# Eighty-row loads, batch 2 with paired local loads and padded keys, and a new order, in a sparse attention and ELU expert kernel

## The chip, the cores and the metric

The kernel runs on one core of a Trainium2 chip. The core has five engines with a queue each: TensorE (PE) multiplies matrices, VectorE (DVE) and ScalarE (ACT) work element by element, GpSimd (POOL) here mostly issues the loads, and SyncE (SP) issues the transposing copies and the stores. The metric is the time of the whole kernel on the device in microseconds (us), the median over its runs; lower is better.

## The reference

Attention over 8 batches, 8 heads, 576 positions of 64 numbers, in float32. The first four heads see the last 32 positions, the other four every position of the same residue modulo 32. The result goes through two layers with an ELU between them.

```python
scores = (q @ k.T) / sqrt(64)
local   = (rel >= 0) & (rel < 32)                        # heads 0 to 3
strided = (rel >= 0) & (pos_k % 32 == pos_q % 32)        # heads 4 to 7
x = softmax(where(mask, scores, -1e9)) @ v               # 4608 tokens x 512
h = x @ w_in                                             # 512 x 2048
g = where(h > 0, h, exp(min(h, 0)) - 1)
out = g @ w_out                                          # 2048 x 512
```

## The kernel before

**Attention.** A position is split into a residue of 8 (NS) and one of 72 rows (RS). A unit of attention is a pair of heads: `0s1` is batch 0, strided, pair 1; `2l0` is batch 2, local, pair 0. Each pair goes through two halves (u = 0, 1), and each step of it is a token of the text ORDER:
- `l.` load of q, k or v by POOL, cast to bf16 (`qs`, `ks`, `vs` strided, `ql`, `kl`, `vl` local, then the batch, and a or b for half the heads); `wi`, `wo` are quarters of the two weights
- `T` transposes on PE (line 370), `c` and `C` the copies of their result out of PSUM by DVE or ACT (line 386); `D` and `K`, instead of these, the transposing copy on SP (line 557) and the copy into padded keys (line 568)
- `S` scores (line 399), `e` the exponential on ACT, `m` the mask on DVE, `O` the product with v (line 494), `n` the logarithm of the sums, `r` its negative exponential (both ACT), `x` the scaled result into xT (line 524, DVE)
- `A`, `F`, `z` set-up; `V`, `W` copies of v; `w` idle matmuls on zeros that fill PE.

A token's last number names PSUM banks: there are eight in all, and a token that writes a bank waits for the last reader of what lay there before.

**Three kinds of batch.** Batches 0, 1 and 2 (PE_T) have their transposes on PE; there the scores of the two pair members use half of the array's rows each (`Pair.rows`). For their local heads, one transpose of half width is made for each head and each of the 8 residues: 16 a token. Batches 3 to 7 use D and K: q lies in qTs, qTl, shared by all batches; k in kTs, kTl and from there in kps, kpl, in which the other head's rows are zero, so that the scores use all rows. A batch's D.qs thus waits for the last scores of the batch before. D.qs needs 80 rows (RP) for 72; the set-up A.r (line 320) fills the 8 spare rows once. Batches 0 and 1 add the sums by products with ones (`pv_old`); batches 2 to 7 take them along with v (V_ONES).

**The two layers.** Tokens go in 9 chunks of 512. For each of 16 slices m: `a` and `b` (or `L`) are the four matmuls of layer 1 (line 574), `h` the exponential on ACT, `i` (DVE) or `j` (ACT) the clamp, `g` the ELU's join on DVE. Layer 2 is `Z`, four matmuls a token (line 609); `o` (ACT) or `q` (DVE) copies the result, `t` stores it. Layer 1 of chunk 0 starts with the strided half of x (`a`) and adds the local half (`b`).

**What sets the order.** ORDER is written out in full by a planner and executed token by token; each engine gets its instructions in that order and waits only for the data it needs. SP's queue holds D, K and t, POOL's all loads.

Of the kernel before, what the change touches and what calls it, by code (L numbers as in the profile page):

```python
# [9 lines left out]
BF16 = mybir.dt.bfloat16  # L10
# [6 lines left out]
D = 64  # L17
# [14 lines left out]


# [7 lines left out]
A.i w.7.34 l.ks0b z.1 l.qs0b F.0 A.p F.2 l.qs0a z.0 l.ks0a z.2 l.kl0 F.1 T.0s1.k.0 w.7.5 A.m  # L41
l.ql0 C.0s1.k T.0s1.q.1 l.vs0 w.7.5 z.3 C.0s1.q l.vl0 T.0s0.q.0 w.7.1 C.0s0.q S.0s1.0.23
S.0s1.1.45 l.wi0 e.0s1.0 T.0s0.k.0 w.7.15 e.0s1.1 m.0s1.0 l.wo1 C.0s0.k m.0s1.1 l.wi1 T.0l1.k.1
l.wi2 S.0s0.1.67 c.0l1.k T.0l0.k.0 l.vs1 e.0s0.1 S.0s0.0.23 C.0l0.k m.0s0.1 l.wi3 T.0l1.q.1
e.0s0.0 A.l T.0l0.q.7 C.0l1.q m.0s0.0 w.6.3 O.0s1.0.2345 C.0l0.q O.0s1.1.2345 S.0l0.0.01 n.0s1
S.0l1.0.67 r.0s1 l.wo0 e.0l1.0 x.0s1 e.0l0.0 l.ks1 S.0l0.1.67 m.0l1.0 S.0l1.1.23 m.0l0.0 l.qs1
e.0l0.1 O.0s0.0.0145 V.0 e.0l1.1 O.0s0.1.0145 l.ql1 m.0l0.1 m.0l1.1 O.0l1.0.2367 n.0s0 l.qs2
r.0s0 O.0l1.1.2367 l.kl1 x.0s0 n.0l1 l.vl1 r.0l1 O.0l0.0.0145 O.0l0.1.0145 l.wo2 x.0l1 n.0l0
l.wo3 a.0.0.2 r.0l0 a.0.1.3 l.ks2 a.0.2.6 x.0l0 a.0.3.7 l.ql2 l.vs2 b.0.0 b.0.1 l.kl2 h.0.0
a.0.4.0 h.0.1 b.0.2 i.0.0 l.vl2 g.0.0 b.0.3 h.0.2 b.0.4 j.0.2 a.0.5.2 a.0.6.1 j.0.1 g.0.2 b.0.5  # L50
h.0.4 g.0.1 b.0.6 h.0.5 a.0.7.6 i.0.4 b.0.7 h.0.6 i.0.5 a.0.8.3 g.0.4 h.0.7 b.0.8 g.0.5 h.0.3
a.0.9.0 i.0.7 b.0.9 h.0.8 g.0.7 a.0.10.2 h.0.9 b.0.10 i.0.3 j.0.8 g.0.3 a.0.11.6 a.0.12.4 h.0.10
g.0.8 b.0.11 j.0.10 i.0.6 b.0.12 i.0.9 h.0.11 a.0.13.3 g.0.9 a.0.14.7 h.0.12 g.0.10 b.0.13
j.0.12 b.0.14 g.0.6 j.0.11 a.0.15.2 g.0.12 b.0.15 h.0.14 T.1s0.k.5 g.0.11 j.0.14 T.1s0.q.4
c.1s0.k T.1s1.k.1 h.0.15 g.0.14 T.1s1.q.6 C.1s0.q Z.0.0.0.5 c.1s1.q h.0.13 i.0.15 c.1s1.k
S.1s0.0.67 g.0.15 S.1s0.1.01 e.1s0.0 i.0.13 T.1l1.q.4 e.1s0.1 g.0.13 S.1s1.1.67 c.1l1.q
T.2s1.q.0 m.1s0.1 e.1s1.1 S.1s1.0.12 m.1s0.0 T.2s0.q.4 c.2s1.q e.1s1.0 O.1s0.1.67 l.qs3 m.1s1.1
C.2s0.q m.1s1.0 O.1s0.0.01 A.r n.1s0.1 T.1l1.k.2 r.1s0.1 O.1s1.1.34 n.1s0.0 x.1s0.1 Z.0.0.1.5
r.1s0.0 C.1l1.k x.1s0.0 T.1l0.k.6 n.1s1.1 V.1 S.1l1.1.01 r.1s1.1 c.1l0.k T.1l0.q.2 e.1l1.1
x.1s1.1 O.1s1.0.67 c.1l0.q S.1l1.0.01 m.1l1.1 n.1s1.0 S.1l0.0.34 r.1s1.0 Z.0.0.2.5 e.1l1.0  # L60
x.1s1.0 e.1l0.0 m.1l1.0 S.1l0.1.67 O.1l1.1.01 m.1l0.0 e.1l0.1 O.1l1.0.23 n.1l1.1 m.1l0.1
O.1l0.0.67 n.1l1.0 Z.0.0.3.5 r.1l1.0 r.1l1.1 x.1l1.0 Z.0.1.0.4 n.1l0.0 x.1l1.1 o.0.0 T.2s1.k.0
r.1l0.0 Z.0.1.1.4 t.0.0 C.2s1.k x.1l0.0 Z.0.1.2.4 Z.0.1.3.4 O.1l0.1.23 q.0.1 Z.0.2.0.0 l.vl3
n.1l0.1 t.0.1 r.1l0.1 T.2s0.k.1 W.2 Z.0.2.1.0 l.ks3 C.2s0.k x.1l0.1 Z.0.2.2.0 l.vs3 Z.0.2.3.0
Z.0.3.0.1 q.0.2 Z.0.3.1.1 t.0.2 Z.0.3.2.1 Z.0.3.3.1 V.2 L.1.0.0 q.0.3 L.1.1.2 t.0.3 h.1.0
S.2s1.1.56 i.1.0 h.1.1 g.1.0 S.2s0.0.34 e.2s1.1 L.1.2.1 i.1.1 e.2s0.0 m.2s1.1 L.1.3.0 g.1.1
h.1.2 m.2s0.0 O.2s1.1.56 h.1.3 S.2s0.1.34 i.1.2 g.1.2 L.1.4.2 n.2s1.1 i.1.3 r.2s1.1 L.1.5.1
g.1.3 h.1.4 x.2s1.1 T.2l0.q.7 h.1.5 i.1.4 O.2s0.0.56 e.2s0.1 c.2l0.q T.2l0.k.0 g.1.4 n.2s0.0
S.2s1.0.34 m.2s0.1 r.2s0.0 L.1.6.2 D.qs c.2l0.k e.2s1.0 x.2s0.0 L.1.7.7 h.1.6 m.2s1.0 D.ks
O.2s0.1.34 i.1.5 h.1.7 S.2l0.0.56 g.1.5 L.1.8.0 n.2s0.1 i.1.7 r.2s0.1 g.1.7 T.2l1.q.1 e.2l0.0  # L70
x.2s0.1 T.2l1.k.7 l.ql3 h.1.8 m.2l0.0 O.2s1.0.56 c.2l1.q L.1.9.3 n.2s1.0 c.2l1.k K.s L.1.10.1
r.2s1.0 i.1.8 g.1.8 h.1.9 L.1.11.7 x.2s1.0 h.1.10 l.kl3 L.1.12.0 i.1.9 h.1.11 g.1.9 O.2l0.0.45
i.1.10 L.1.13.6 n.2l0.0 g.1.10 L.1.14.3 r.2l0.0 i.1.6 g.1.6 l.ks4 h.1.13 L.1.15.1 x.2l0.0 j.1.13
l.qs4 i.1.11 S.2l1.1.45 h.1.15 g.1.11 Z.1.0.0.2 e.2l1.1 i.1.15 g.1.13 h.1.14 S.2l1.0.45 m.2l1.1
h.1.12 S.2l0.1.67 i.1.14 Z.1.0.1.2 e.2l1.0 D.kl i.1.12 g.1.14 e.2l0.1 O.2l1.1.45 g.1.12
Z.1.0.2.2 n.2l1.1 D.ks m.2l0.1 S.3s0.1.67 r.2l1.1 g.1.15 e.3s0.1 x.2l1.1 O.2l0.1.01 D.ql n.2l0.1
S.3s0.0.67 m.3s0.1 S.3s1.0.34 m.2l1.0 Z.1.0.3.2 e.3s0.0 W.3 e.3s1.0 m.3s0.0 Z.1.1.0.7 l.kl4 K.l
q.1.0 r.2l0.1 O.3s0.1.56 m.3s1.0 O.3s0.0.34 t.1.0 x.2l0.1 n.3s0.1 Z.1.1.1.7 n.3s0.0 V.3
O.2l1.0.01 Z.1.1.2.7 r.3s0.0 r.3s0.1 l.vl4 x.3s0.0 Z.1.1.3.7 n.2l1.0 x.3s0.1 Z.1.2.0.2 l.vs4
r.2l1.0 q.1.1 O.3s1.0.34 l.ks5 x.2l1.0 S.3s1.1.56 t.1.1 n.3s1.0 Z.1.2.1.2 l.ql4 r.3s1.0 D.qs  # L80
S.3l0.0.01 L.2.0.7 e.3l0.0 x.3s1.0 e.3s1.1 m.3l0.0 L.2.1.0 K.s h.2.0 m.3s1.1 L.2.2.1 h.2.1 i.2.0
g.2.0 j.2.1 O.3s1.1.34 S.3l1.1.56 h.2.2 L.2.3.7 g.2.1 e.3l1.1 L.2.4.0 j.2.2 m.3l1.1 D.kl n.3s1.1
L.2.5.5 g.2.2 r.3s1.1 L.2.6.6 h.2.4 x.3s1.1 l.qs5 L.2.7.1 h.2.6 i.2.4 g.2.4 h.2.3 L.2.8.3 h.2.7
i.2.3 L.2.9.0 g.2.3 h.2.8 i.2.7 h.2.5 L.2.10.4 i.2.6 h.2.9 g.2.6 Z.1.2.2.2 j.2.9 i.2.5 g.2.7
h.2.10 S.3l1.0.67 Z.1.2.3.2 g.2.9 e.3l1.0 g.2.5 j.2.10 O.3l1.1.01 S.3l0.1.67 V.4 n.3l1.1
Z.1.3.0.5 K.l g.2.10 e.3l0.1 Z.1.3.1.5 m.3l1.0 r.3l1.1 m.3l0.1 O.3l0.0.67 o.1.2 x.3l1.1
Z.1.3.2.5 n.3l0.0 t.1.2 W.4 O.3l0.1.01 r.3l0.0 Z.1.3.3.5 i.2.8 l.vs5 n.3l0.1 x.3l0.0 L.2.11.2
r.3l0.1 q.1.3 O.3l1.0.67 D.ks x.3l0.1 h.2.11 L.2.12.4 l.vl5 n.3l1.0 i.2.11 L.2.13.5 g.2.11
# [24 lines left out]
x.5l0.1 L.4.9.3 h.4.8 i.4.7 t.3.3 L.4.10.0 g.4.7 j.4.8 K.s h.4.9 g.4.8 L.4.11.1 h.4.10 i.4.9
L.4.12.2 i.4.10 h.4.11 g.4.10 j.4.11 O.5s1.1.56 g.4.9 L.4.13.4 n.5s1.1 W.6 L.4.14.3 r.5s1.1
# [47 lines left out]
def kernel(  # L162
# [71 lines left out]
    def rawof(nm, b):  # L234
        return (raw1 if b == 1 else raw)[nm]
# [444 lines left out]
```

## Time and profile before

| | |
|---|---|
| median of 13 runs | 327.97 us (326.53 to 332.23) |
| the profiled execution | 326.53 us, its span 324.8 us |
| DVE, ACT busy | 228.9, 239.5 us |
| loads (q0) | 18.48 MB |
| transposes, K and stores (q1) | 18.95 MB |
| mean granted TensorE clock | 0.972 |
| end of the last matmul | 320.72 us |

A row of the timeline names start and length in us, engine, line, and how many instructions it merges; what stands in brackets is idle time before it and what ended it. A matmul's own duration (380 ns for 512 columns) is longer than the time from its start to the next one's start (216 ns), as they are pipelined; only the second can be added up. The landing of the loads is issue to last byte, so it holds the wait in the queue.

### The profile page before, as it was taken

What the parts mean: (1) busy time and instruction counts of PE and PEld (TensorE: products, weight loads), DVE (VectorE), ACT (ScalarE), POOL (GpSimd) and SP (SyncE); (2) the same over time, 40 slices, a digit from 0 to 9 for tenths busy, and PEclk for the clock granted to TensorE, in tenths of its full rate; (3) what the DMA queues carried; (4) which work ended last, traced back from release to release, by engine and by line L of the source; (5) the groups of instructions that cost most, each with busy time, mean ns of one, the idle gap of its engine ahead of it and who ended that gap; (6) DMA issues with size and microseconds to landing.
All of it is one profiled execution on the core that took longest, in us unless ns stands there. A gap on an engine that the chain in (4) does not pass through costs nothing.

```text
span 324.8 us, 6336 instructions
## 1 busy us (share of the span) xinstructions
PE 305.2 (94%) x2392; PEld 161.1 (50%) x2431; DVE 228.9 (70%) x423; ACT 239.5 (74%) x413; POOL 75.8 (23%) x105
## 2 busy tenths in 40 slices
PE   7869989989799999999999999998999999999994
PEld 6754554444355455554555444554544544444442
DVE  6655994399997999659686998854489569495010
ACT  3695986199798999789799988954898878592101
POOL 8753341305455041050513360000000000000000
PEclk9558999999999999999999999999999999999999
DMA  6999999937999999979999998129200210200332
GB/s 82 170 206 205 187 200 194 143 85 139 129 173 179 149 146 158 174 155 131 145 139 148 185 143 77 59 79 185 66 2 1 67 32 0 67 0 0 93 104 66
DMA packets 95663, 37.84 MB, mean 116 GB/s; under 512 B 76912, under 2 KB 89744, under 8 KB 95632
## 3 DMA queue, kind: packets, MB, share of 16 engines
q0 software_dynamic: 62576, 18.48, 55.2%
q1 hardware_dynamic: 33056, 18.95, 28.1%
q8 instruction: 19, 0.31, 0.4%
q14 instruction: 12, 0.10, 0.1%
HBM read 36.90 MB, written 9.44 MB: 143 GB/s over the span
## 4 chain that ended last, share of the span: by engine, by line
PE 61%; DVE 20%; ACT 9%; issue 4%; DMA 3%; POOL 1%; SPq 1%; ACTq 0%; POOLq 0%; DVEq 0%
PE ps L613 29%; PE ps L579 24%; DVE g L607 6%; DVE he L596 4%; ACT ln L516 3%; DVE g L605 3%; PE ps L418 3%; DVE xT L547 3%; ACT rc L522 2%; DMA kl<-in_k_dram 2%; PE ps L481 1%; ACT e L425 1%; DMA qTs<-qs 1%; PE ps L488 1%; DVE pm L438 1%
## 5 line engine op out<-in xcount | busy, mean ns | idle before, releaser
L579 PE MATMUL ps<-xT,w_in_sb 128*128 128x512 bf16 x560 | 130.5, 382 | 2.7 <-DVE g L607 0.7
L613 PE MATMUL ps<-w_out_sb,g 128*128 128x512 bf16 x553 | 131.2, 379 | 1.4 <-issue 0.3
L587 ACT ACTIVATE he<-ps 128x512 f32<-128x512 f32 x144 | 81.4, 591 | 23.2 <-PE ps L579 21.7
L579 PEld LDWEIGHTS <-w_in_sb 128*128 128x128 bf16 x576 | 55.5, 98 | 67.8 <-issue 6.0
L613 PEld LDWEIGHTS <-g 128*128 128x128 bf16 x576 | 53.1, 98 | 56.0
L607 DVE TENSOR_TENSOR g<-he,ps 128x512 bf16<-128x512 bf16 x89 | 60.5, 686 | 2.3
L547 DVE TENSOR_TENSOR xT<-ps,rc 64x576 bf16<-64x576 f32 (+2 forms) x60 | 42.7, 714 | 27.0 <-ACT rc L522 26.3
L425 ACT ACTIVATE e<-ps 72x576 bf16<-72x576 f32 (+1 forms) x64 | 39.9, 645 | 11.3 <-PE ps L418 10.6
L516 ACT ACTIVATE ln<-ps 64x576 f32<-64x576 f32 (+2 forms) x60 | 36.6, 613 | 13.4 <-PE ps L488 5.7
L596 DVE TENSOR_SCALAR he<-he 128x512 bf16<-128x512 f32 x89 | 37.9, 435 | 9.3 <-ACT he L587 8.9
L605 DVE SCALAR_TENSOR_TENSOR g<-he,ps 128x512 bf16<-128x512 bf16 x55 | 36.9, 683 | 7.6 <-ACT he L594 7.3
L522 ACT ACTIVATE rc<-ln 64x576 f32<-64x576 f32 (+2 forms) x60 | 38.8, 649 | 1.7
L594 ACT ACTIVATE he<-he 128x512 bf16<-128x512 f32 x55 | 34.1, 628 | 1.2
L619 DVE COPY osb<-ps 128x512 f32<-128x512 f32 x19 | 13.1, 688 | 27.9 <-PE ps L613 25.6
L619 ACT COPY osb<-ps 128x512 f32<-128x512 f32 x17 | 10.0, 586 | 24.7 <-PE ps L613 24.4
L248 POOL DMA_DIRECT2D ql<-in_q_dram x20 | 16.2, 816 | 26.6 <-PE ps L382 16.9
L255 POOL DMA_DIRECT2D kl<-in_k_dram x20 | 15.2, 776 | 17.9 <-DMA kTl<-kl 17.9
L432 DVE TENSOR_TENSOR pm<-e,mask_s 72x576 bf16<-72x576 bf16 x32 | 14.1, 449 | 4.2 <-ACT e L425 4.1
L438 DVE TENSOR_TENSOR pm<-e,mask_l 128x576 bf16<-128x576 bf16 x32 | 14.3, 454 | 3.4 <-ACT e L425 2.9
L263 POOL DMA_DIRECT2D vl<-in_v_dram x8 | 9.8, 1228 | 14.8 <-PE ps L466 6.5
L481 PEld LDWEIGHTS <-vsp 72*128 72x128 bf16 x192 | 9.1, 98 | 5.0 <-issue 0.4
L488 PEld LDWEIGHTS <-vl 128*128 128x128 bf16 x144 | 8.6, 96 | 5.4 <-issue 1.3
(84 smaller groups left out, 185.1 us busy)
## 6 DMA issues: line engine op xcount, KB each, us to landing
out_dram<-osb SPq DMA_DIRECT2D x32, 144.0 KB
vl<-in_v_dram POOLq DMA_DIRECT2D x8, 288.0 KB, 8.9
w_in_sb<-in_moe_w_in_dram POOLq DMA_DIRECT2D x4, 512.0 KB, 15.9
w_out_sb<-in_moe_w_out_dram POOLq DMA_DIRECT2D x4, 512.0 KB, 14.7
vs<-in_v_dram POOLq DMA_DIRECT2D x7, 288.0 KB, 8.9
qs<-in_q_dram POOLq DMA_DIRECT2D x6, 288.0 KB, 7.6
ks<-in_k_dram POOLq DMA_DIRECT2D x6, 288.0 KB, 8.0
kps<-kTs SPq DMA_DIRECT2D x10, 160.0 KB
```

Source lines behind the costliest of these rows:

```text
L425: nc.scalar.activation(e[0:R], tiles.pop(("S", key, u))[0:R], ACT.Exp, scale=scale)
L516: nc.scalar.activation(t, s_ps, ACT.Ln)
L522: nc.scalar.activation(t, tiles.pop(("ln", key, u)), ACT.Exp, scale=-1.0)
L547: nc.vector.tensor_mul(dst, o_ps, rc)
L579: nc.tensor.matmul(tiles["h", ch, m], lhsT=w_in_sb[:, c, m * 128:(m + 1) * 128], rhs=xT[:, c, ch * CHUNK:(ch + 1) * CHUNK], start=(c == 2) ...
L587: nc.scalar.activation(e, tiles["h", i[0], i[1]], ACT.Exp)
L594: nc.scalar.activation(e1, e, ACT.Relu, bias=1.0, scale=-1.0)
L596: eng.tensor_scalar(e1, e, scalar1=1.0, scalar2=1.0, op0=ALU.min, op1=ALU.subtract)
L605: nc.vector.scalar_tensor_tensor(dst, e1, -1.0, h, op0=ALU.mult, op1=ALU.max)
L607: nc.vector.tensor_tensor(dst, e1, h, op=ALU.max)
L613: nc.tensor.matmul(ops, lhsT=g[ch % 2][:, m, kk * 128:(kk + 1) * 128], rhs=w_out_sb[:, m, :], start=(m == 0), stop=(m == MC - 1), skip_gro ...
L619: eng(o_sb, tiles.pop(("o", int(ch), int(kk))))
```

## The change

- Long loads of q, k, v take 80 rows (RP) where the source has that many behind it; only the last batch's strided ones keep 72. The 8 rows more hold the first rows of the next head and are read as nothing but filler. A.r goes.
- Batch 2 (PE_SIDE): its local q and k are loaded in pieces of 64 numbers, with two heads side by side, so that one transpose serves two heads: 8 for q, 6 for k.
- Batch 2 (PE_PAD): the copies after its k transposes go straight into the padded kps and kpl, one for each of the two heads; its scores use all rows.
- Batch 0's strided and local products go into two banks for each half instead of four for both, so `n`, `r`, `x` come once for each half.
- ORDER is new throughout. Batch 0 starts with strided pair 0; its copies are all DVE's; the loads come in another order; batch 2's attention begins during chunk 0's layer 2. Chunk 8 is begun before chunk 7.

```diff
+PE_SIDE = (2,)
+PE_PAD = (2,)
...
-A.i w.7.34 l.ks0b z.1 l.qs0b F.0 A.p F.2 l.qs0a z.0 l.ks0a z.2 l.kl0 F.1 T.0s1.k.0 w.7.5 A.m
-l.ql0 C.0s1.k T.0s1.q.1 l.vs0 w.7.5 z.3 C.0s1.q l.vl0 T.0s0.q.0 w.7.1 C.0s0.q S.0s1.0.23
...
-r.0s0 O.0l1.1.2367 l.kl1 x.0s0 n.0l1 l.vl1 r.0l1 O.0l0.0.0145 O.0l0.1.0145 l.wo2 x.0l1 n.0l0
-l.wo3 a.0.0.2 r.0l0 a.0.1.3 l.ks2 a.0.2.6 x.0l0 a.0.3.7 l.ql2 l.vs2 b.0.0 b.0.1 l.kl2 h.0.0
...
-Z.4.3.3.7 O.6l0.1.01 q.4.3 S.6s1.0.45 n.6l0.1 S.6l1.0.23 K.s Z.5.0.0.6 e.6s1.0 Z.5.0.1.6 r.6l0.1
-D.ql m.6s1.0 e.6l1.0 x.6l0.1 Z.5.0.2.6 m.6l1.0 t.4.3 O.6s1.0.45 Z.5.0.3.6 n.6s1.0 W.7 D.qs
-Z.5.1.0.7 r.6s1.0 o.5.0 x.6s1.0 O.6l1.0.23 Z.5.1.1.7 K.l n.6l1.0 Z.5.1.2.7 r.6l1.0 t.5.0 x.6l1.0
-Z.5.1.3.7 S.7s0.1.01 q.5.1 Z.5.2.0.2 e.7s0.1 t.5.1 S.7l1.1.45 m.7s0.1 Z.5.2.1.2 e.7l1.1
...
+A.i w.7.35 l.qs0a F.1 l.ks0a z.2 z.1 A.p l.qs0b z.0 l.ks0b z.3 l.vs0 F.2 T.0s0.q.0 w.7.3 l.ql0
+c.0s0.q T.0s0.k.1 F.0 w.7.8 l.kl0 c.0s0.k l.vl0 A.m T.0s1.q.0 S.0s0.0.23 c.0s1.q S.0s0.1.45 A.l
+e.0s0.0 w.7.3 T.0s1.k.0 e.0s0.1 m.0s0.0 w.7.12 c.0s1.k m.0s0.1 S.0s1.1.67 O.0s0.0.12 e.0s1.1
+S.0s1.0.34 n.0s0.0 m.0s1.1 l.wi0 O.0s0.1.56 e.0s1.0 T.0l0.q.7 l.wi1 n.0s0.1 m.0s1.0 O.0s1.1.34
+r.0s0.0 c.0l0.q l.wi2 r.0s0.1 T.0l1.q.0 x.0s0.0 n.0s1.1 x.0s0.1 l.wi3 T.0l1.k.7 r.0s1.1 c.0l1.q
+x.0s1.1 O.0s1.0.12 l.qs1 c.0l1.k T.0l0.k.0 n.0s1.0 l.ks1 r.0s1.0 w.6.1 c.0l0.k S.0l1.0.56 l.vs1
+S.0l1.1.34 e.0l1.0 x.0s1.0 w.7.3 l.wo0 V.0 S.0l0.0.01 e.0l1.1 m.0l1.0 S.0l0.1.56 l.wo1 e.0l0.0
+m.0l1.1 w.7.1 O.0l1.0.23 e.0l0.1 l.ql1 m.0l0.0 O.0l1.1.01 n.0l1.0 m.0l0.1 l.kl1 O.0l0.0.45
+r.0l1.0 O.0l0.1.67 x.0l1.0 l.vl1 n.0l0.0 r.0l0.0 a.0.0.2 n.0l0.1 x.0l0.0 a.0.1.3 l.wo2 r.0l0.1
+a.0.2.4 n.0l1.1 x.0l0.1 l.wo3 a.0.3.5 r.0l1.1 a.0.4.6 x.0l1.1 l.qs2 a.0.5.7 b.0.0 l.vl2 b.0.1
...
+T.2s0.k.0 t.0.1 O.1l1.0.23 c.2s0.k0 O.1l0.0.56 C.2s0.k1 Z.0.2.1.7 l.vl3 n.1l0.0 W.2 r.1l0.0
+S.2s0.1.01 Z.0.2.2.7 x.1l0.0 e.2s0.1 l.vs3 n.1l1.0 S.2s0.0.45 m.2s0.1 Z.0.2.3.7 e.2s0.0 r.1l1.0
...
+D.ql x.6l0.0 Z.5.0.0.7 e.6s1.1 V.7 e.6l1.1 O.6l1.0.01 m.6s1.1 S.6s1.0.56 Z.5.0.1.7 t.4.3 m.6l1.1
+e.6s1.0 n.6l1.0 O.6s1.1.23 K.s m.6s1.0 O.6l1.1.45 Z.5.0.2.7 n.6l1.1 D.qs Z.5.0.3.7 r.6l1.1
+r.6l1.0 x.6l1.1 Z.5.1.0.6 K.l n.6s1.1 x.6l1.0 O.6s1.0.45 r.6s1.1 Z.5.1.1.6 q.5.0 n.6s1.0 x.6s1.1
+Z.5.1.2.6 t.5.0 r.6s1.0 W.7 S.7s0.1.01 S.7s1.0.23 x.6s1.0 e.7s0.1 Z.5.1.3.6 e.7s1.0 m.7s0.1
...
     raw["kl"] = consts.tile([LQ, HG * NS * D], BF16, tag="kl", name="kl")
-    raw["vs"] = consts.tile([RS, HG * NS * D], BF16, tag="vs", name="vs")
-    raw1 = {nm: xT[0:RS, i, n_tokens - HG * NS * D:]
+    raw["vs"] = consts.tile([RP, HG * NS * D], BF16, tag="vs", name="vs")
+    raw1 = {nm: xT[0:raw[nm].shape[0], i, n_tokens - HG * NS * D:]
             for i, nm in enumerate(("qs", "ks", "ql", "kl"))}
-    raw1["vs"] = g[1][0:RS, 0:HG * NS * D // CHUNK, :].rearrange("p a b -> p (a b)")
+    raw1["vs"] = g[1][0:RP, 0:HG * NS * D // CHUNK, :].rearrange("p a b -> p (a b)")
...
         x = {"q": q, "k": k, "v": v}[nm[0]]
-        t = rawof(nm, b)
         hb = (HG if nm[1] == "s" else 0) + h0
+        rows = RP if b * H + hb + n < B * H else RS
         nc.gpsimd.dma_start(
-            out=t[0:RS].rearrange("p (h f) -> p h f", h=HG)[:, h0:h0 + n],
-            in_=x[b, hb:hb + n].rearrange("h (p s) d -> p h (s d)", s=NS))
+            out=rawof(nm, b)[0:rows].rearrange("p (h f) -> p h f", h=HG)[:, h0:h0 + n],
+            in_=bass.AP(x.tensor, x[b, hb].offset,
+                        [[NS * D, rows], [S * D, n], [1, NS * D]]))
+    def side(b, h):
+        return (h % 2, h // 2) if b in V_ONES else (h // 2, h % 2)
     def load_qloc(b):
-        t = raw["ql"].rearrange("p (y s x d) -> p y s x d", y=2, s=NS, x=2)
+        t = rawof("ql", b).rearrange("p (y s x d) -> p y s x d", y=2, s=NS, x=2)
         for h in range(HG):
-            nc.gpsimd.dma_start(
-                out=t[0:RS, h % 2, :, h // 2, :],
-                in_=q[b, h].rearrange("(p s) d -> p s d", s=NS))
+            y, x = side(b, h)
+            nc.gpsimd.dma_start(out=t[0:RS, y, :, x, :],
+                                in_=q[b, h].rearrange("(p s) d -> p s d", s=NS))
     def load_kloc(b):
-        t = raw["kl"][:, 0:HG * LB * D].rearrange("p (y t x d) -> p y t x d", y=2, t=LB, x=2)
+        t = rawof("kl", b)[:, 0:HG * LB * D].rearrange("p (y t x d) -> p y t x d", y=2, t=LB, x=2)
         for h in range(HG):
-            nc.gpsimd.dma_start(
-                out=t[:, h % 2, :, h // 2, :],
-                in_=k[b, h].rearrange("(t p) d -> p t d", p=LQ))
+            y, x = side(b, h)
+            nc.gpsimd.dma_start(out=t[:, y, :, x, :],
+                                in_=k[b, h].rearrange("(t p) d -> p t d", p=LQ))
...
             load_runs(nm, b, 2 * "ab".index(half), 2)
-        elif nm[1] == "l" and b not in PE_T:
+        elif nm[1] == "l" and (b not in PE_T or b in PE_SIDE):
             (load_qloc if nm[0] == "q" else load_kloc)(b)
...
             nc.vector.memset(ones, 1.0)
-            nc.vector.memset(kT["l"][:, 0:PRE], 0.0)
+            nc.vector.memset(
+                kT["l"][:, 0:2 * S].rearrange("c (y n) -> c y n", y=2)[:, :, 0:PRE], 0.0)
         elif what == "p":
...
                                            op1=ALU.mult)
-        elif what == "l":
+        else:
...
                 nc.gpsimd.memset(blocks(t, HG * LB)[0:PRE, 0, :], 0.0)
-        else:
-            for nm, x in (("qs", q), ("ks", k), ("ql", q)):
-                nc.gpsimd.dma_start(
-                    out=raw[nm][RS:RP].rearrange("p (h f) -> p h f", h=HG),
-                    in_=x[0, 0:HG].rearrange("h (p s) d -> p h (s d)", s=NS)[0:RP - RS])
...
         nc.vector.memset(t[(1 - z) * D:(2 - z) * D, :], 0.0)
-        s_ = slice(2 * NS * RP, None) if c == "s" else slice(0, PRE)
-        nc.vector.memset(t[z * D:(z + 1) * D, s_], 0.0)
+        if c == "s":
+            pad = t[z * D:(z + 1) * D, 2 * NS * RP:]
+        else:
+            pad = t[z * D:(z + 1) * D, 0:2 * S].rearrange("c (y n) -> c y n", y=2)[:, :, 0:PRE]
+        nc.vector.memset(pad, 0.0)
...
             self.vone = self.b in V_ONES
+            self.tile = self.pe and self.b not in PE_PAD
             self.str = self.c == "s"
...
         def rows(self, z):
-            return slice(z * D, (z + 1) * D) if self.pe else slice(0, 128)
+            return slice(z * D, (z + 1) * D) if self.tile else slice(0, 128)
...
         tiles["T", key, nm] = t
-        src = rawof(nm + P.c, P.b)[0:RS].rearrange("p (h f) -> p h f", h=HG)
+        src = rawof(nm + P.c, P.b)
+        if P.b in PE_SIDE and not P.str:
+            n, w = (NS, RS) if nm == "q" else (LB, LQ)
+            for i in range(n):
+                c0 = (P.y * n + i) * 2 * D
+                nc.tensor.transpose(t[:, i * w:(i + 1) * w], src[0:w, c0:c0 + 2 * D],
+                                    identity[0:w, 0:w])
+            return
+        src = src[0:RS].rearrange("p (h f) -> p h f", h=HG)
         for i in range(NS):
...
-    def copy_T(eng, key, nm):
-        P = Pair(key)
-        t = tiles.pop(("T", key, nm))
+    def copy_T(eng, key, what):
+        P, nm = Pair(key), what[0]
+        if what == "k1" or what in "qk":
+            t = tiles.pop(("T", key, nm))
+        else:
+            t = tiles["T", key, nm]
+        rows, to = slice(0, 128), qT if nm == "q" else kT
+        to = to[P.c]
+        if what[1:]:
+            z = int(what[1])
+            rows, to = slice(z * D, (z + 1) * D), kp[P.c, z]
+        to, t = to[rows], t[rows]
         if P.str:
-            dst = (qT if nm == "q" else kT)["s"][:, 0:2 * S].rearrange("c (h n) -> c h n", h=HG)
             h0, dh = P.head(0), P.head(1) - P.head(0)
+            dst = to[:, 0:2 * S].rearrange("c (h n) -> c h n", h=HG)
             eng(dst[:, h0:h0 + dh + 1:dh], t.rearrange("c (x n) -> c x n", x=2))
         elif nm == "q":
-            eng(qT["l"][:, P.q0:P.q0 + S], t)
-        else:
-            eng(kT["l"][:, PRE + P.k0:PRE + P.k0 + S].rearrange("c (p s) -> c p s", s=NS),
+            eng(to[:, P.q0:P.q0 + S], t)
+        elif P.b in PE_SIDE:
+            eng(to[:, PRE + P.k0:PRE + P.k0 + S], t)
+        else:
+            eng(to[:, PRE + P.k0:PRE + P.k0 + S].rearrange("c (p s) -> c p s", s=NS),
                 t.rearrange("c (s p) -> c p s", s=NS))
...
                 pr = P.rows(z)
-                kt = kT[P.c] if P.pe else kp[P.c, z]
+                kt = kT[P.c] if P.tile else kp[P.c, z]
                 if P.str:
...
         nc.vector.tensor_copy(blocks(vs_p, HG * NS),
-                              raw["vs"].rearrange("p (n d) -> p n d", d=D))
+                              rawof("vs", int(b))[0:RS].rearrange("p (n d) -> p n d", d=D))
...
```

## The prediction, made before the changed kernel was run

> **What bounds it now.** First the page's busy rows and slices, then TensorE's (PE's) timeline, then the windows.
>
> ```profile
> PE 305.2 (94%) x2392; PEld 161.1 (50%) x2431; DVE 228.9 (70%) x423; ACT 239.5 (74%) x413; POOL 75.8 (23%) x105
> ...
> PEclk9558999999999999999999999999999999999999
> ```
>
> PE is the bound on average, but busy is not work: its clock is at half in slices 2 and 3. So I count its work: each token of the order times the start-to-start time of its rows at full clock. Four 512-column matmuls take 0.865 us; a scores or new-form output token 0.26 (0.22 to 0.23 for scores at half height); old-form outputs 0.38 strided, 0.27 local; 8 strided transposes 0.26, 16 half-width ones 0.38. From the first layer-1 matmul (a.0.0.2) to the last, the order before has 283.3 us.
>
> ```profile
> 23.41 0.59 PE L579 MATMUL ps<-xT,w_in_sb 128*128 128x512 bf16 x1 [0.46 <-DVE xT L547]
> ...
> 63.80 1.89 PE L579 MATMUL ps<-xT,w_in_sb 128*128 128x512 bf16 x8
> ...
> 99.72 2.79 PE L579 MATMUL ps<-xT,w_in_sb 128*128 128x512 bf16 x12
> ...
> 292.93 27.79 PE L613 MATMUL ps<-w_out_sb,g 128*128 128x512 bf16 x125
> ```
>
> These rows are a.0.0.2, the first of chunk 1 (L.1.0), the first of chunk 2 (L.2.0), and the last run. The end, 320.7, is 297.3 after 23.4: **14.0 us of PE are lost** after the head. By stretch: 23.4 to 63.8 is 40.4 for 35.7 of work (4.7 lost, some 1.5 of it half clock); 63.8 to 99.7 is 35.9 for 30.0 (5.9 lost); the rest loses 3.3. Why the second?
>
> ```profile
> 60.00:80.00 20.00, 18.38 (x196) 9.74 (x199) 16.14 (x31) 13.98 (x24) 3.09 (x4) 1.00 0.74 115
> 80.00:100.00 20.00, 17.57 (x162) 9.46 (x163) 18.55 (x34) 16.51 (x28) 11.84 (x16) 1.00 1.31 159
> ```
>
> The third busy number is VectorE (DVE): 18.55 of 20, while PE has 17.57. Multiplying the tokens of that stretch by the by-form durations:
>
> ```profile
> L607 DVE TENSOR_TENSOR g<-he,ps 128x512 bf16<-128x512 bf16 x89 | 60.5, 686 | 2.3
> ...
> L596 DVE TENSOR_SCALAR he<-he 128x512 bf16<-128x512 f32 x89 | 37.9, 435 | 9.3 <-ACT he L587 8.9
> L547 DVE TENSOR_TENSOR xT<-ps,rc 64x576 bf16<-64x576 f32 x48 | 36.1, 754 | 20.8 <-ACT rc L522 20.1
> ```
>
> 16 g x 0.685, 15 i x 0.435, 10 x x 0.754, 11 masks x 0.45, and copies, make 35.7 us of DVE against 30.0 of PE and 31.8 of ScalarE (ACT). The stretch took 35.9: DVE set it. In the stretch before, DVE has 29.5 for 35.7 of PE: room was left, then missed.
>
> **The change, part by part.** *TensorE.* Batch 2's local transposes go from 4 x 16 to 2 x (8 + 6), 0.38 to 0.26 a token: -0.48 us. Full height in its scores costs 14 tokens x 0.03 or 0.04: about +0.3. With 3 more warm-up matmuls the work after a.0.0.2 is 283.1: **-0.2, nothing**.
>
> *Batch 2's copies.* k is copied twice, 64 rows each, into the padded tiles: 4 more copies at about 0.45 (the contiguous DVE copies of 128x576), while two strided ones (0.744) become contiguous: +1.2 us, spread over two stretches and counted below. What is gained is that batch 3's k transposes no longer wait for batch 2's reads of kTs, kTl.
>
> *Loads.* The three pad loads (A.r, 96 KB, 1.7 us of POOL) go; nothing waits for them within 20 us. Batch 2's local q, k become 8 issues (0.816, 0.776 us) for 2 (0.71): +5 us on POOL. Behind them stands l.vl3, due 20 us of PE work later: hidden. Eighty rows for 72 are 11% more bytes in the long loads. Here a rule and rows part:
>
> ```profile
> 4.00:6.00 2.00, 1.91 (x23) 1.64 (x21) 1.79 (x2) 0.34 (x1) 2.00 (x4) 1.00 1.04 133
> 6.00:8.00 2.00, 0.87 (x21) 0.70 (x20) 1.36 (x5) 0.94 (x2) 2.00 (x3) 1.00 1.16 140
> ...
> 30.00:32.00 2.00, 2.00 (x11) 0.88 (x9) 2.00 (x5) 1.79 (x4) 0.74 (x2) 1.00 1.24 205
> ```
>
> The last two numbers are DMA share and GB/s. With 72-row loads the engines are nearly as busy (1.04 to 1.16) as with weights (1.24) yet move 140 for 205. The Trainium skill (DMA: Bandwidth & Descriptors, "Why a DMA increments its semaphore by 16 and not by 1") takes the largest count up to 16 that divides the rows: 12 engines for 72, 16 for 80, so 5 rows an engine for 6, 17% less; it adds that some such loads were measured with 16 engines and rows rounded up, where 72 and 80 both give 5 and nothing is won. By the rule kl0 lands some 2 us earlier; by the rows, with several loads in flight and engines busy, the 11% of bytes eats what little is free. I take the rows: rate unchanged. kl0 then comes seventh of the loads at 1.64 MB, about 17 us (it landed at 11.7); by the rule 14.7. The copies of the strided part keep DVE to about 18 anyway, so the difference is under 0.7 us.
>
> *The head.* Before, ACT is full from 14 to 23 us with 7 copies (0.64), 8 exponentials and pairs of log and reciprocal. Now all 8 copies are DVE's, but the pairs go by half (0.406 + 0.442, 8 pairs). DVE's chain, by the memset rows of before (z 0.62 to 0.69, F.0 and F.1 1.45, F.2 1.87, 0.2 to 0.4 between them): z and F.1, F.2 to 7.9, first copy 8.4, F.0, second copy 10.6, scores, first exponential 10.9 (before: 8.8). ACT then needs 8 x 0.645 = 5.2 and, up to the x that frees bank 2, 5 half pairs = 4.2; it waits 1.4 for scores behind PE's fillers and 0.9 for kl's copy (18.7); x takes 0.45: a.0.0.2 comes at **23.1** (23.4 before); bounds 21.5 (no waits) and 24.5 (kl0 2 us late). The following a-tokens are released one by one, at half clock, as before: no more is gained.
>
> *The order.* The same count for after, PE / DVE / ACT: a.0.0.2 to L.1.0 34.7 / 33.0 / 32.6 (before 35.7 / 29.5 / 30.3); L.1.0 to L.2.0 **30.5 / 30.3 / 29.6** (before 30.0 / 35.7 / 31.8). Batch 2's attention starts in chunk 0's layer 2, and DVE's surplus of 5.7 us is gone.
> - Stretch 1: DVE still runs over where batch 1 starts (14.2 us in 10 of PE, before 13.5), and the DMA is tight: from wi0 on, 6.1 MB at 205 put wo3 at 49 us, due at 49. I take 5.7 lost: 40.4, the same as before.
> - Stretch 2: three nearly equal engines. The nearest row is before's stretch L.2.0 to L.3.0 (21.1 / 21.1 / 21.9), which lost about 1; I take 1.5: 32.0 (bounds 30.5 and 35), before 35.9.
> - The rest: 217.9 of work; loss 4.3 against 3.3, for two reasons. Between 135 and 177 us of work DVE has 43.6 for 42. And the hand-overs of qTs are short:
>
> ```profile
> 221.96 0.02 SPq L561
> ...
> 222.01 3.76 DMA qTs<-qs
> ...
> 225.81 0.42 PE ps L418 x8
> ```
>
> From the last read of qTs, batches 5, 6 and 7 now have 5.4, 5.1 and 6.2 us of PE work before their first scores. They need K.s's issue (1.2) and this transpose (3.8): 5 to 6.5 with loads beside it. Before, only batch 7 was late, by 1.3 us (8 us, but behind stores and D.ql on SP). I take 1.5 for the three; bounds 0 and 4.
>
> Tail as before: 4.1 us from the last matmul. **Sum:** 23.1 + 40.4 + 32.0 + 222.2 + 4.1 = **321.8**, against 324.8. The profiled run took 326.5, 1.7 more than its span, and the median is 1.4 above that run: 321.8 + 3.2 = **325.0 us**.
>
> **Rivals.**
> - *The plan holds (18%).* Head 21.8, stretch 2 at 30.7, the later DVE surplus absorbed (-1.2): 321.8 - 1.3 - 1.3 - 1.2 = 318.0, time **321.2**. For it: DVE and ACT have room in every neighbouring stretch. Against it: in no stretch before did equal engines lose nothing.
> - *The load queue takes over (17%), the slow side.* One queue brings, in order, batch 0 (now 11% larger), weights, batch 1, wo2, wo3; in the order after, kl1 (42.5), wo2, wo3 and qs2 each come within a microsecond or so of their use. At 38 to 44 us the trace moved only 171 to 176 GB/s, with small pieces. At 175 for 205 the 6.1 MB take 35 us for 30: PE stands 5 us at Z.0.0.3 and nothing later returns it. It decides from 3 us late on. Time 325.0 - 0.5 + 5 = **329.5**, slower. Against it: before, the same weights were in time.
> - *Hand-overs (10%).* Each of the three is 1 to 2 us late: 325.0 - 1.5 + 3 to 6, middle **328.0**. For it: the 3.8 us were without loads beside them; against it: whatever PE loses between the two places lengthens the lead.
> - *Eighty rows do nothing*: that is already in the forecast.
>
> **Numbers.** The forecast has 55% (own range 322.5 to 327.5). Less than 0.5%, 1.6 us, can't be told from no change here: faster is under 326.3, slower over 329.6. Forecast: 46 faster, 7 same, 2 slower; the plan holds: 18 faster; load queue: 4, 4, 9; hand-overs: 4, 3, 3. Together 0.72, 0.14, 0.14. The range 320 to 329 leaves out part of the plan's best case and the worst of the load queue.
>
> **What would show it.** Right: L.1.0 to L.2.0 falls from 35.9 to about 32, with DVE no longer fuller than PE there; a.0.0.2 near 23; total matmul work unchanged; GB/s in 4 to 10 us still near 140. Wrong: a wait of PE on w_out_sb, kl or xT loads over 2 us near 40 to 55 us; PE waits on qTs, kps over 1.5 us at three places; GB/s in the head near 170 with the first exponential before 10 us.

## The result, and the profile after

| | before | after |
|---|---|---|
| median | 329.58 us (48 runs, the 13 of above among them) | **323.94 us** (322.17 to 327.97, 11 runs) |
| ratio to before | 1 | **0.988**, 95% interval 0.984 to 0.991 |
| profiled execution, its span | 326.53, 324.8 | 324.44, 322.7 |
| DVE, ACT busy | 228.9, 239.5 | 238.4, 235.9 |

The forecast was 325.0. Ratios leave out disturbed runs, in which the whole kernel is some per cent slower, and medians do not, so the one is not always the quotient of the other; the profiles of two experiments (no masks, the move alone) are of such runs, and of these only stretch 2 is read, where the clock is whole. The page's busy rows and slices of after:

```profile
PE 304.6 (94%) x2359; PEld 161.7 (50%) x2398; DVE 238.4 (74%) x441; ACT 235.9 (73%) x411; POOL 77.3 (24%) x108
...
PE   6789989999999999999999997999999999999994
...
PEclk9559989999999999999999999999999999999999
```

DVE has 9.5 us more to do in all, and the kernel is faster: what matters is where the work stands. A new digit in PE's row, the 7 in slice 25, is a wait that before does not have. The timeline's rows of the same four marks as before (a.0.0.2, chunk 1, chunk 2, the last run):

```profile
23.82 0.59 PE L608 MATMUL ps<-xT,w_in_sb 128*128 128x512 bf16 x1
...
63.97 1.67 PE L608 MATMUL ps<-xT,w_in_sb 128*128 128x512 bf16 x7
...
94.38 2.97 PE L608 MATMUL ps<-xT,w_in_sb 128*128 128x512 bf16 x13
...
292.44 26.06 PE L642 MATMUL ps<-w_out_sb,g 128*128 128x512 bf16 x118
```

Chunk 1's row holds seven of its eight matmuls; with the missing one in front it begins at 63.75. Chunk 2 begins at 94.35, the last matmul ends at 318.5. Against the forecast, in us:

| stretch | before | forecast | after |
|---|---|---|---|
| start to a.0.0.2 | 23.4 | 23.1 | 23.8 |
| 1: to chunk 1 (L.1.0) | 40.4 | 40.4 | 39.9 |
| 2: to chunk 2 (L.2.0) | 35.9 | 32.0 | **30.6** |
| rest, to the last matmul | 221.0 | 222.2 | 224.1 |
| tail | 4.1 | 4.1 | 4.2 |
| span | 324.8 | 321.8 | 322.7 |

Stretch 2 gave 5.3 us and the rest took 3.1 back. Two windows, first before, then after, show stretch 2 whole (busy time of PE, PEld, DVE, ACT and POOL, then the clock, the DMA share and GB/s):

```profile
63.80:99.72 35.92, 31.92 (x338) 17.36 (x342) 33.37 (x61) 30.24 (x50) 14.65 (x19) 1.00 0.96 138
```

```profile
63.75:94.35 30.60, 30.32 (x259) 16.75 (x261) 27.74 (x53) 27.94 (x47) 15.86 (x20) 1.00 1.18 130
```

The clock is whole (1.00) in both. In after, PE is busy for 30.32 of 30.60 us, with DVE and ACT below 28. Nothing to speak of is lost there; the stretch now lasts as long as its matmuls.

Of the 3.1 us that the rest took back, one wait makes up 1.9. It is the largest of PE's waits in after that before does not have in its place:

```profile
PE ps L447 <- DMA qTl<-ql: 1.9, 1, 1.9
```

(us in total, times, longest.) The experiments ask: does the order or the code bring the gain; was DVE what set stretch 2; what delays qTl; what do eighty rows do. A fifth asks what a half clock in mid-kernel costs. Ratios are always to the kernel before on the same chip.

### The profile page after: what moved, and what is told of

Read it like the earlier page. It is cut to its first block, busy times and chain, and to the rows that moved or that the text cites. A ratio compares the mean times of both kernels' runs of the same rounds, so it can differ in the third digit from the quotient of the medians.

```text
span 322.7 us, 6299 instructions
## 1 busy us (share of the span) xinstructions
PE 304.6 (94%) x2359; PEld 161.7 (50%) x2398; DVE 238.4 (74%) x441; ACT 235.9 (73%) x411; POOL 77.3 (24%) x108
## 4 chain that ended last, share of the span: by engine, by line
PE 64%; DVE 17%; DMA 7%; ACT 6%; issue 3%; SPq 1%; DVEq 0%; ACTq 0%
PE ps L642 30%; PE ps L608 25%; DVE g L636 6%; PE ps L447 4%; DMA qTl<-ql 4%; DVE he L625 4%; DVE g L634 2%; DMA kps<-kTs 2%; ACT e L454 2%; ACT ln L545 2%; ACT rc L551 1%; PE ps L510 1%; PE ps L517 1%; DVE xT L576 1%; DMA qTs<-qs 1%
## 5 line engine op out<-in xcount | busy, mean ns | idle before, releaser
L642 PE MATMUL ps<-w_out_sb,g 128*128 128x512 bf16 x555 | 133.6, 381 | 1.6 <-issue 0.4
L576 DVE TENSOR_TENSOR xT<-ps,rc 64x576 bf16<-64x576 f32 (+1 forms) x64 | 43.2, 679 | 22.4 <-ACT rc L551 21.0
L545 ACT ACTIVATE ln<-ps 64x576 f32<-64x576 f32 (+1 forms) x64 | 37.3, 584 | 9.0 <-PE ps L510 3.3
L551 ACT ACTIVATE rc<-ln 64x576 f32<-64x576 f32 (+1 forms) x64 | 39.4, 620 | 1.8
L648 DVE COPY osb<-ps 128x512 f32<-128x512 f32 x25 | 17.2, 687 | 18.6 <-PE ps L642 18.1
L648 ACT COPY osb<-ps 128x512 f32<-128x512 f32 x11 | 6.4, 586 | 31.8 <-PE ps L642 31.8
L260 POOL DMA_DIRECT2D ql<-in_q_dram x24 | 19.9, 833 | 28.5 <-DMA qTl<-ql 16.2
L267 POOL DMA_DIRECT2D kl<-in_k_dram x24 | 18.3, 772 | 28.7 <-DMA kTl<-kl 23.1
L447 PEld LDWEIGHTS <-kpl 128*128 128x128 bf16 x144 | 8.4, 97 | 6.8 <-issue 2.5
L447 PE MATMUL ps<-qTl,kpl 128*128 128x96 bf16 x144 | 9.9, 205 | 2.0 <-DMA qTl<-ql 1.9
```

Source lines behind the costliest of these rows:

```text
L447: nc.tensor.matmul(dst[0:M], lhsT=kt[pr, k0:k0 + M], rhs=rhs, start=True, stop=True, skip_group_check=True)
L545: nc.scalar.activation(t, s_ps, ACT.Ln)
L551: nc.scalar.activation(t, tiles.pop(("ln", key, u)), ACT.Exp, scale=-1.0)
L576: nc.vector.tensor_mul(dst, o_ps, rc)
L642: nc.tensor.matmul(ops, lhsT=g[ch % 2][:, m, kk * 128:(kk + 1) * 128], rhs=w_out_sb[:, m, :], start=(m == 0), stop=(m == MC - 1), skip_gro ...
```

## Experiments

**The code under the old order.** After's code, with ORDER of before; the only tokens that change are those that the code needs:

```diff
-... O.1s0.0.01 A.r n.1s0.1
+... O.1s0.0.01 n.1s0.1
-... C.2s1.k ... C.2s0.k ... c.2l0.k ... c.2l1.k ...
+... C.2s1.k0 C.2s1.k1 ... C.2s0.k0 C.2s0.k1 ... c.2l0.k0 c.2l0.k1 ... c.2l1.k0 c.2l1.k1 ...
```

> The changed kernel's code (80-row loads, paired local loads and padded keys for batch 2) under the order of before; only batch 2's k copies become two each. Theory (the gain is the order's balance of VectorE): the stretch from chunk 1's first matmul to chunk 2's keeps its 35.9 us or grows by up to 1.5 with the added copies; ratio to before 0.997 to 1.006. Rival (loads and padded keys bring the gain): ratio 0.992 or less, with a shorter head or stretch.

331.31 us, ratio 1.006 (1.002 to 1.009). Stretch 2 took 35.8 us (66.53 to 102.36). So the gain comes with the order; paired loads, padded copies and eighty rows alone cost about half a per cent. Of the profiles here, all eight with the new order have stretch 2 at 30.4 to 31.3 us, before and this run at 35.8 to 35.9. That the code is the means by which batch 2 can start earlier is argued and not shown: no run has the new order with the old code, and the parts of the order were not run one by one.

**Does DVE set stretch 2?** Before's kernel without batch 2's eight masks:

```diff
-        e = tiles["e", key, u] = p_e.tile([128, 2, W], BF16, tag="e", name="e")
+        if P.b == 2:
+            e = tiles["pm", key, u] = p_pm.tile([128, 2, W], BF16, tag="pm", name="pm")
+        else:
+            e = tiles["e", key, u] = p_e.tile([128, 2, W], BF16, tag="e", name="e")
...
+        if P.b == 2:
+            return
```

> The kernel before without the masks of batch 2 (its exponential is used unmasked, so batch 2's output is another): 8 VectorE instructions of 0.45 us fewer, all between chunk 1's first matmul and chunk 2's. Theory (VectorE sets this stretch: 35.7 of its 35.9 us): the stretch falls by about 3.5 us to 32 to 33, and most of it stays in the end: 321 to 322 for a span of 324.8, ratio 0.989 to 0.992. Rival (the stretch waits for transposed copies and loads, VectorE is only fuller there): it falls by less than 1 us.

330.68 us, ratio 0.994 (0.990 to 0.998): a gain of half a per cent, where about one was expected. The stretch as a whole did not shrink. Its window, in that kernel:

```profile
68.67:104.76 36.09, 31.70 (x343) 17.20 (x342) 30.86 (x54) 30.26 (x50) 16.08 (x20) 1.00 0.98 138
```

DVE has 30.86 instead of 33.37, and the stretch is 36.09 instead of 35.92. But the length of the whole hides two changes. The last scores of batch 3 on its strided keys (kps) and the first on its local ones (kpl), just ahead of chunk 2, first in before, then in this kernel:

```profile
98.33 0.43 PE L418 MATMUL ps<-qTs,kps 128*128 128x72 bf16 x8
...
99.46 0.42 PE L418 MATMUL ps<-qTl,kpl 128*128 128x96 bf16 x6
```

```profile
101.64 0.43 PE L418 MATMUL ps<-qTs,kps 128*128 128x72 bf16 x8
...
104.10 0.22 PE L418 MATMUL ps<-qTl,kpl 128*128 128x96 bf16 x1 [1.16 <-DMA kpl<-kTl]
```

From the start of chunk 1 to the first of the two rows, before takes 34.53 us and this kernel 32.97: 1.56 less for 2.5 us of DVE. From there to chunk 2 before takes 1.39 us and this kernel 3.12, with a wait for kpl. The chain of waits of this kernel at this place (start, length, what):

```profile
88.14 7.02 DMA ks<-in_k_dram
...
95.17 1.33 SPq L566
...
96.67 1.33 SPq L566
...
98.88 5.61 DMA kpl<-kTl
...
104.54 0.39 PE ps L418 x5
```

Read from the end: the scores wait for K.l, the copy of batch 3's local keys. That one, and D.ql before it, stood in SP's queue behind D.ks of batch 4 (95.17), which waited 1.7 us for batch 4's ks to be loaded; the load took 7.0 us here and 5.4 in before, for a reason that no view shows. A transposing copy for the next batch blocks one that is due now. In before D.ks did not have to wait, kpl landed at 98.22, and PE did not wait for it; but it landed only 1.2 us ahead of its first use, so that little time is saved by reaching it earlier.

To take the second change away, the blocking token was moved, once in before and once in the kernel without the masks:

```diff
-... n.2l1.1 D.ks m.2l0.1 ... Z.1.1.0.7 l.kl4 K.l
+... n.2l1.1 m.2l0.1 ... Z.1.1.0.7 l.kl4 K.l D.ks
```

> The kernel before with one token moved: batch 4's D.ks goes from ahead of batch 3's D.ql to right behind batch 3's K.l, so that SP no longer stands on batch 4's ks load while batch 3's q and k are wanted. If DVE alone sets the stretch from chunk 1's first matmul to chunk 2's: it stays at 35.9 us, within 0.5, and the time is unchanged. If the hand-over of batch 3 alone sets it: 33 us and 2 to 3 us faster. If both are equally long: unchanged here, and shorter only with the masks gone as well (next run).

> The same move, and batch 2's eight masks left out as well (its exponential writes the tile that the mask would have written, so batch 2's output differs). Without the masks alone the stretch was 36.1 us. If DVE and batch 3's hand-over are two chains of about the same length: with both cut the stretch falls to 32 to 34 us and the time by 1.5 to 3 us against the kernel before. If neither sets it: still near 36 us, and something else does.

The move alone: 329.44 us, ratio 1.001 (0.997 to 1.005). Move and no masks: 328.00, ratio 0.996 (0.993 to 0.999). Stretch 2 in the two windows, the move alone first:

```profile
68.30:103.84 35.54, 32.18 (x343) 17.34 (x342) 32.83 (x61) 30.23 (x50) 12.74 (x16) 1.00 1.05 138
```

```profile
67.44:101.79 34.35, 31.35 (x343) 17.21 (x342) 30.42 (x53) 30.08 (x50) 13.14 (x16) 1.00 0.96 127
```

Cut at the same scores (with both edits they start at 100.41), in us:

| | stretch 2 | chunk 1 to last scores on kps | from there to chunk 2 |
|---|---|---|---|
| before | 35.92 | 34.53 | 1.39 |
| no masks | 36.09 | 32.97 | 3.12 |
| move alone | 35.54 | 34.16 | 1.38 |
| both | 34.35 | 32.97 | 1.38 |

Without the masks the first part falls by 1.56 us, with the move or without it, and the move removes the late kpl. The times go with that: the masks are worth about half a per cent in both kernels, the move alone nothing that can be measured. So DVE did hold PE back, for 1.6 us of the 2.5 taken from it. Batch 3's hand-over was close behind but set nothing in before.

34.35 is still above the 32 to 34 expected, and 4.3 above the stretch's work. In this kernel PE waits some ten times for 0.3 to 0.7 us, nearly always for DVE or ACT (g, x, e and pm), which neither edit removes; of before's 3.5 us of PE's waits there, 3.3 are put down to DVE. The new order removes them all at once: after's waits list none for this stretch. DVE here still has 30.42 us to do where after has 27.74, and no run took so much away under the old order, so how the last 4 us divide between DVE's amount of work and the place of each instruction is not shown.

**What delays qTl.** The chain of waits of after at this place:

```profile
188.36 11.94 DMA qTl<-ql
...
200.43 0.43 PE ps L447 x6
```

D.ql of batch 6 took 11.94 us to land. POOL's and SP's timelines say what ran beside it:

```profile
186.06 0.73 POOL L247 DMA_DIRECT2D vs<-in_v_dram  x1 [12.18 <-DVE vsp L583]
186.93 0.72 POOL L247 DMA_DIRECT2D qs<-in_q_dram  x1
190.17 1.20 POOL L274 DMA_DIRECT2D vl<-in_v_dram  x1 [2.53 <-PE ps L447]
...
188.36 3.67 SPq L590 DMA_TRANSPOSE qTl<-ql  x1
192.14 4.59 SPq L590 DMA_TRANSPOSE kTs<-ks  x1
```

Three loads of batch 7, whose scores come only after 220 us, run beside it. So they were moved behind the load that waits for qTl in any case:

```diff
-... e.5l0.1 l.vs7 Z.4.1.1.5 ... O.5l1.1.01 l.qs7 e.5l1.0 ... q.4.1 l.vl7 Z.4.2.0.4 ... h.5.3 l.ql7 h.5.2
+... e.5l0.1 Z.4.1.1.5 ... O.5l1.1.01 e.5l1.0 ... q.4.1 Z.4.2.0.4 ... h.5.3 l.ql7 l.vs7 l.qs7 l.vl7 h.5.2
```

> The changed kernel with the loads of vs, qs and vl of batch 7 put behind that of ql of batch 7 in the load queue, which waits for the transposed qTl of batch 6. Theory (that transpose took 11.9 us instead of some 4 because these three loads ran beside it, and PE stood 1.9 us for it): it lands in under 7 us, PE's wait for qTl is gone, and the time falls by 1 to 2 us (ratio to before 0.981 to 0.985). Rival (the transpose is slow by the two other transposes and the stores, or the loads now come too late for batch 7): the wait stays or moves to batch 7, and the time is the changed kernel's or above.

> The kernel after with batch 7's three last loads moved behind its local q, the same kernel as before, taken again, since its interval was wide: 0.979 to 0.987 if batch 6's late local transpose was worth the 2 us that it waited; 0.988 as after if other things fill that time.

First 323.31 us, ratio 0.983 (0.979 to 0.987); again 322.36, ratio **0.978** (0.972 to 0.983), lower than after's 0.984 to 0.991. The wait for qTl is gone in both profiles; it stands, with 0.6 to 1.9 us, in all six profiles of the new order with these loads in the old place, where the copy takes 9.9 to 11.9 us to land. Here it landed in 5.0 and 4.5 us. The same two entries of SP's timeline, now in this kernel, and POOL's load that waits for the landing (the first of the two runs):

```profile
187.19 1.33 SPq L587 DMA_TRANSPOSE qTl<-ql  x1
188.63 2.69 SPq L587 DMA_TRANSPOSE kTs<-ks  x1
...
192.82 3.39 POOL L257 DMA_DIRECT2D ql<-in_q_dram  x4 [19.52 <-DMA qTl<-ql]
```

That load starts 5.6 us after the transpose's issue; in after it is 12.6 (200.92 after 188.36). Even SP's own time for the transpose fell, 3.67 to 1.33 us. The load queue, which the forecast watched at the start of the kernel, does harm here by being too early. This version clearly beats before, and likely after: one of its two intervals lies just below after's, the other overlaps it, and no run had the two side by side.

**Eighty rows.** First after with 72 rows everywhere (A.r comes back once, as the transposes read 80 rows), taken twice; then 72 rows for k and v of batches 0 to 2 only, and of 3 to 7 only:

```diff
-        rows = RP if b * H + hb + n < B * H else RS
+        rows = RS
```

```diff
+        rows = RP if (b > 2 or nm[0] == "q") and b * H + hb + n < B * H else RS
```

```diff
+        rows = RP if b * H + hb + n < B * H and (b < 3 or nm[0] == "q") else RS
```

> The changed kernel with its long loads cut back to 72 rows, the 8 spare rows of qs, ks and ql filled once. Theory (the engines were busy all the same, so 80 rows bring 11% more bytes and no more rate): kl0 lands no later than with 80 rows (15.1 us), the rate from 4 to 10 us stays 125 to 150 GB/s, and the time is that of the changed kernel within 0.4%. Rival (72 rows use 12 engines, 80 use 16): each early load takes about a fifth longer, kl0 lands 2 us later, and the time is 1 us or more above the changed kernel's.

> The kernel after with 72-row loads everywhere, the same kernel as in the first run, taken again. If its 0.994 is its own: 0.991 to 0.997 again, with the wait for kps near 131 us. If a hole in the DMA by chance: near 0.988, without the wait.

> The kernel after, with 72 rows again for the long loads of k and v of batches 0 to 2 only (q and all later ones keep 80). If eighty rows gain nothing in the head, as forecast, and what they gain lies at the later hand-overs: time as after, ratio 0.985 to 0.990, no wait of PE on kps over 1 us. If the gain is in the first loads: like 72 rows everywhere, ratio 0.992 to 0.996.

> The other half of the run before last: the kernel after with 72 rows for the long loads of k and v of batches 3 to 7 only. If what eighty rows gain lies at the later hand-overs, because these loads and the copies of K share the engines: ratio 0.992 to 0.996 as with 72 rows everywhere, and PE waits for kps at batch 5 for over 1 us again. If the hole at 125 to 127 us in the profile with 72 rows everywhere (the DMA moved 21 to 27 GB/s there while a copy was under way) was a single event: no such wait, kps landing in about 6 us, and a ratio of 0.986 to 0.989 as after.

| 72 rows in | ratio | kps of batch 5 landed in | PE waited there |
|---|---|---|---|
| everywhere | 0.994 (0.991 to 0.997) | 8.90 us | 3.6 us |
| everywhere, again | 0.990 (0.982 to 0.997) | 7.15 | 2.0 |
| batches 3 to 7, k and v | 0.987 (0.983 to 0.992) | 9.05 | 3.1 |
| batches 0 to 2, k and v | 0.986 (0.981 to 0.991) | 5.55 | 0.3 |
| none (after) | 0.988 (0.984 to 0.991) | 5.76 | 0.2 |

The profiles agree: the late wait comes with the later 72-row loads in three of three, and is not there in the one profile with only the first loads at 72 rows. With eighty rows in batches 3 to 7 the five profiles (after, 72 early, fillers, late batch 7 twice) show 0 to 1.3 us of wait, and kps lands in 5.3 to 6.4 us against 7.2 to 9.1. The windows at this place, with 72 rows everywhere and then in after:

```profile
124.00:126.00 2.00, 2.00 (x18) 1.04 (x16) 1.71 (x3) 1.94 (x4) 0.65 (x1) 1.00 1.76 111
126.00:128.00 2.00, 2.00 (x11) 0.88 (x9) 1.45 (x2) 0.10 (x1) 0.08 (x1) 1.00 0.37 88
```

```profile
124.00:126.00 2.00, 2.00 (x22) 1.05 (x19) 1.56 (x3) 1.94 (x4) 0.53 (x1) 1.00 1.22 222
126.00:128.00 2.00, 1.95 (x10) 0.93 (x10) 1.65 (x4) 1.04 (x2) 0.82 (x2) 1.00 1.74 234
```

With 72 rows the DMA moved 111 and 88 GB/s, with a share of only 0.37 in the second window, while K.s was under way. But single microseconds as empty are found with eighty rows too (a share of 0.23 and 33 GB/s from 126 to 127 us with 72 early, 0.48 and 25 from 129 to 130 with fillers), so such a hole does not tell the two apart. Why the copy lands later beside the 72-row loads, no view shows. In the medians the difference is not settled: the first run with 72 rows everywhere barely touches after's interval, the second lies across it, and the kernel with the late wait has the ratio of after. At most some 0.6% can be hidden there.

**Fillers against the half clock.** TensorE's granted clock is at half from 46 to 49 us in after, not in before. Just ahead of that, PE is busy for 0.40 of a microsecond (43 to 44). Twelve idle matmuls were put there:

```diff
-... e.1s0.1 g.0.15 T.1l1.q.4 e.1s1.0
+... e.1s0.1 g.0.15 w.4.12 T.1l1.q.4 e.1s1.0
```

> The kernel after with 12 idle matmuls on zeros in front of the transposes of batch 1's local q at about 43 us, where PE was busy 0.40 of a us and the clock then fell to half from 46 to 49 us. If that gap brings the half clock: 46 to 49 us at full clock, chunk 1 begins up to 1.6 us earlier, ratio about 0.983. If the half clock comes for another reason: it is still there, and the fillers cost up to 0.5 us.

325.02 us, ratio 0.989 (0.985 to 0.993): no gain. The windows of after, and then with fillers:

```profile
38.00:48.00 10.00, 8.82 (x140) 4.87 (x140) 9.83 (x21) 8.52 (x18) 3.29 (x6) 0.90 1.53 194
```

```profile
38.00:48.00 10.00, 9.43 (x150) 5.36 (x148) 9.83 (x20) 8.74 (x18) 2.83 (x4) 1.00 1.58 192
```

The clock is whole. Chunk 1 still begins at 63.75, with a.0.0.2 at 23.87: 39.9 us in both. DVE is busy for 9.83 of 10 us either way: there PE waits for DVE, and at half clock it only waits less. The half clock here, where another engine sets the pace, cost nothing that can be measured. That the gap brings it is not shown: five of the seven profiles of the new order without fillers have the half clock, all with such a gap (0.34 to 0.63 busy), but the other two, one of the late batch 7 and one with 72 rows, had the same gap (0.37 and 0.38) and a whole clock.

## Why the prediction was right, step by step

The direction and the size hold: 325.0 against 323.94, with the gain in stretch 2 as named. But the sum was right partly by offsetting errors.

- **TensorE's work, unchanged.** It holds: stretch 2 took 30.6 for a count of 30.5.
- **Stretch 2, 32.0 by an allowance of 1.5 for three equal engines.** Too high by 1.4: nothing was lost. The DVE count was too high: 30.3 against 27.74 busy, as 35.7 was for before against 33.37. Three rows of DVE's timeline of before show why:

```profile
72.09 0.68 DVE L607 TENSOR_TENSOR g<-he,ps 128x512 bf16<-128x512 bf16 x1
72.69 0.45 DVE L432 TENSOR_TENSOR pm<-e,mask_s 72x576 bf16<-72x576 bf16 x1
73.06 0.75 DVE L396 COPY kTl<-ps 128x576 bf16<-128x576 bf16 x1
```

  The second starts 0.60 us after the first, which lasts 0.68, and the third 0.37 after the second, which lasts 0.45: neighbours overlap, and counts times durations exceed the busy time by 7 to 9%. I had set PE's matmuls right for this and not DVE's.
- **"The stretch took 35.9: DVE set it."** Half right. The 35.7 that made DVE look full for the whole stretch was too high by 2.3 (33.37 busy), so it was busy for 93% of the time and not all of it. DVE did hold PE back: 2.5 us less of it gave 1.6, where the forecast's reading would have given nearly all. It was not alone: batch 3's hand-over had only 1.2 us to spare, and came late, for a loss of 1.7, in the profile without the masks. The size of the gain, 5.3 us, came out because the new order ended PE's waits altogether; which part of it DVE's smaller share of work brought is not known.
- **Batch 2's copies, "what is gained is that batch 3's k transposes no longer wait".** No gain of its own is shown: before's list of waits has none of PE for these transposes either, and the code without the order is at 1.006. Whether the order needs the freedom was not run.
- **The head, 23.1.** 23.8, inside the bounds of 21.5 and 24.5; DVE's chain (two waits of 2.0 and 1.4 us for its copies of q and k) sets it, as worked out.
- **Eighty rows, "rate unchanged, nothing won".** Right for the head. From 4 to 8 us after moved 144 and 151 GB/s, before 133 and 140, but 11% more bytes with it; 72 rows under the new order moved 132 and 130, then 136 and 156, and put a.0.0.2 at 23.9 and 24.1, eighty at 23.8. kl0 landed at 15.1 with eighty rows (9.4 us from its issue) and at 15.3 and 15.1 with 72 (9.1 and 8.9): 17 was too late for either. So the rule of the Trainium skill (DMA: Bandwidth & Descriptors, "Why a DMA increments its semaphore by 16 and not by 1"), by which the forecast estimated 14.7 by way of more engines, is not what brought it early. Later in the kernel "nothing won" failed for the waits: 2.0 to 3.6 us against 0 to 1.3 for K.s of batch 5. The forecast weighed the two readings only on the head's rows, where the DMA share is near 1 all the time.
- **Stretch 1, 5.7 lost.** 5.2 lost. DVE sets it, as forecast. The half clock in it (46.0 to 49.4 us) was not foreseen.
- **The rest, 4.3 lost, of it 1.5 for three short hand-overs of qTs.** 6.2 lost. The qTs waits came to 0.2. The loss was at D.ql of batch 6, which has no place in the sum: I looked at the leads from the last read to the first scores, and not at which loads stand beside each transposing copy. That the term was too small by 1.9, just this wait, is chance: the 1.3 us allowed for qTs and not lost there were lost elsewhere. The stretches with DVE's surplus (135 to 177 us of work) lost the most, 1.9 and 3.0 us, the second with this wait in it.
- **From the span to the median, +3.2.** Taken from before, whose profiled run was the fastest of the first 13; in after it was 1.2. The sum was 0.9 too low and this term 2.0 too high. The two profiled executions differ by 2.1 us, the medians by some 4: profile against profile, the change is worth less than the medians say, and how the rest arises is open.
- **Rivals.** The load queue at the start did not take over: no wait of PE on the weights. The margins were wider than I counted: wo2 and wo3 landed at 44.7 and 47.7 us and were first used 4 and 3 us later, not within about one. Of the hand-overs, one was late by 1.9 us, by another cause than the one given.

## What to carry to other kernels

Before one engine is named as the bound of a stretch, take some of its work away, and then look where in the stretch the time goes: here 1.6 us were won and lost again to a copy that came late at the end, and the length of the whole showed nothing. An instruction for the next batch that waits on an in-order queue delays everything due now that stands behind it (1.7 us in one profile here); follow SP's queue and the loads, not only the busy rows. And a load issued as early as its buffer allows can cost more than it hides, if a transposing copy that is due soon runs beside it.

## What the runs showed of the hardware

The same transposing copy landed in 11.9 us beside three loads (after, qTl of batch 6) and in 5.0 and 4.5 us with these loads moved (late batch 7, twice); its issue alone held SP 3.7 us for 1.3. Beside 72-row loads a copy into padded keys landed in 7.2 to 9.1 us, beside 80-row ones in 5.3 to 6.4; the cause is open. TensorE's clock went to half once more 46 us into the kernel, in five of seven profiles of the new order, and 3.4 us of it cost no measurable time.
